# Preparing the second expert's weights one step a round beside the last chunk's lists, in an attention and mixture-of-experts kernel on one core

## The chip, the cores and the metric
The kernel runs on one core of one Trainium2 chip. The metric is the device time of one execution in microseconds (us), and lower is better. Before the change the median of three runs is 946.49 us (944.94 to 946.53).

## What is computed
The reference is linear attention without a softmax, a normalisation, and a mixture of eight experts of which every row uses two:

```python
kv  = einsum('bhsd,bhse->bhde', k, v)            # 8 batches, 8 heads, 576 rows, 64 wide
out = einsum('bhsd,bhde->bhse', q, kv)
out = out / sqrt(mean(out*out, -1) + 1e-6) * g_norm
x   = out as rows of 512, 4608 of them
noisy = x @ w_gate + log1p(exp(x @ w_noise)) * noise        # 8 logits a row
top2, top2_w = the two largest, softmax over these two
for e in range(8):                                          # w1[e] 512x1024, w2[e] 1024x512
    y[rows of e] += top2_w * (relu(x[rows of e] @ w1[e]) @ w2[e])
```

## The kernel before the change
**Two phases in one instruction stream.** The program is written out in full and every engine runs its instructions strictly in the order in which the Python code issues them (`tc.manual_schedule()`); engines meet at semaphores. In the first phase the attention goes tile by tile (36 tiles of 128 rows); the rows `x` are written to memory (`xs`) and the gate logits are worked out on the way. In the second phase the experts run as *units*: expert 0 has units 0 to 3 of two tiles (256 rows) and a tail, unit 4; every later expert has two units of four tiles (512 rows) and a tail. A unit is a gather of its rows by an indirect DMA from GpSimd (`gather`, L346), transposes into `xT` (`xpose`, L363; for units 0 to 4 by TensorE at L377, evicted by ScalarE at L380 and by VectorE at L381), a first layer (`l1`, L413; matmuls L426, evictions into `hT` by ScalarE L431 and VectorE L432) and a second layer (`l2`, L462; matmuls L470, eviction with the gate by ScalarE L501). Numbers are split into two fp16 halves, so each product takes three matmuls and each eviction writes a high half (ScalarE) and a low half (VectorE).

**Lists.** Which rows belong to an expert is found for chunks of 10, 18, 28 and 36 tiles. For a chunk, `gating` (L132) works out the top two on VectorE, ScalarE and GpSimd and counts rows with matmuls L176 and L178; `onehots` (L290) makes comparison matrices on VectorE (L296, L299, L302); `place` (L306) multiplies them on TensorE (L310); `finish` (L317) turns the result into indices. The units of expert 0 start before all chunks are there: units 0 to 2 (`EARLY` = 3) need only the first three chunks. `locate(1)` (L772) does the same for expert 1's list.

**Weights.** An expert's two weight matrices are loaded (`load_w1` L203, `load_w2` L208), and `weights` (L214) is a generator that prepares them step by step: four absolute-maximum reductions on VectorE (L221, one a step), then a diagonal `dg` (L228), a small fp32 matmul on TensorE that spreads it over the lanes (L232, which waits for `dg`), five short VectorE operations that make the scales (L234 to L241), and for each of four pieces a high half on ScalarE (L246, `w1h`) and a low half on VectorE (L250 and L252, `w1l`). All of this is done for w1 and then for w2. When w1 is split, the load of the next expert's w1 is issued into the same buffer.

**What sets the order around the change.** After the attention loop three things are stepped in rounds, `while side` (L800): `pump` advances the last chunk's lists, `fill_early` advances the early units (here the second layer of unit 1 and the first and second layer of unit 2), and `fill` (L790) advances the first generator of the deque `bg`. `bg` holds `locate(1)` and behind it `prepare(1)` (L763), which runs `weights(1)`. `locate(1)` yields without doing anything once three of its four parts are made, until the last chunk's lists are done, so that `prepare(1)` is not reached in these rounds. Behind the rounds come `finish` for expert 0's remaining tiles, the gathers of units 3 and 4 and their transposes, and then the units one by one.

```python
    bg.append(locate(1))
    bg.append(prepare(1))
    while side:
        pump()
        fill_early()
        fill()
    finish(0, M0, slice(2 * EARLY, CAP))
    gather(EARLY)
```

Of the kernel before, what the change touches and what calls it, by code (L numbers as in the profile page):

```python
# [51 lines left out]
def attention_moe(ctx: ExitStack, tc: tile.TileContext, kvm, kvr, qt, gn, wgn, noise, w1, w2, out):  # L52
# [155 lines left out]
    def load_w2(e):  # L208
        r = RW[e, 1] = late.get("raw", raw).tile([P, 4, 1024], F32, name="rw")
        v = w2[e].rearrange("(c f p) d -> c p f d", f=2, p=P)  # L210
        for c in range(4):
            SP.dma_start(r[:, c].rearrange("p (f d) -> p f d", f=2), v[c])
# [100 lines left out]
    def scale_gates(e, c):  # L313
        if "c" in WT.get(e, ()):
            V.tensor_scalar(LG[e][:, c], LG[e][:, c], WT[e]["c"], None, op0=OP.mult)

    def finish(e, M, c):  # L317
        m = lists.tile([P, 5, CAP], F32, name="m")
        V.tensor_copy(m, M.rearrange("p (v t) -> p v t", v=5))
        a = lists.tile([P, 2, CAP], F32, name="la")  # L320
        V.scalar_tensor_tensor(a[:, 0], m[:, 1], float(P), m[:, 0], op0=OP.mult, op1=OP.add)
        V.tensor_scalar(a[:, 1], m[:, 1], 0.0, lane, op0=OP.is_equal, op1=OP.mult)
        V.tensor_tensor(LI[e][:, c], a[:, 0, c], a[:, 1, c], OP.add)
        V.scalar_tensor_tensor(a[:, 0], m[:, 1], 0.0, sl[:, 1], op0=OP.is_gt, op1=OP.mult)  # L324
        V.tensor_tensor(a[:, 0], a[:, 0], sl[:, 0], OP.add)
        V.tensor_tensor(LS[e][:, c], LI[e][:, c], a[:, 0, c], OP.add)
        V.tensor_tensor(m[:, 2], m[:, 2], m[:, 3], OP.add)
        V.tensor_tensor(LG[e][:, c], m[:, 2, c], m[:, 4, c], OP.add)
        scale_gates(e, c)
# [16 lines left out]
    def gather(u):  # L346
        e, tiles, tail = units[u]
        for t in tiles:
            x = moe_a.tile([P, DM], F32, name="xg", bufs=GB)
            lim = {k // 2 - 1: m for m, k in MARKS.items()}.get(u, NT)  # L350
            src = xs[0:(1 + lim) * P, :]
            G.indirect_dma_start(out=x, out_offset=None, in_=src,  # L352
                                 in_offset=bass.IndirectOffsetOnAxis(ap=LI[e][:, t:t + 1], axis=0))
            XG[u, t] = x
# [179 lines left out]
    with tc.tile_pool(name="p1", bufs=2) as p1, tc.tile_pool(name="ps1", bufs=1, space=PSUM) as ps1:  # L534
# [138 lines left out]
        def pump():  # L673
            for it in list(side):
                it[0] -= 1
                while it[0] <= 0:
                    k = next(it[1], None)
                    if k is None:
                        side.remove(it)
                        break  # L680
                    it[0] = k

        def fill_early():
            while early:
                try:
                    next(early[0])
                    if held[0]:
                        scatter()
                    return
                except StopIteration:  # L690
                    early.popleft()
# [66 lines left out]
    bg = deque()  # L758
# [4 lines left out]
    def prepare(e):  # L763
        yield from weights(e, wts_b if e % 2 else wts_a)
        if e in ready:
            scale_gates(e, slice(0, CAP))
        loaded.add(e)
        if e + 1 < E:
            yield AFT
            load_w2(e + 1)  # L770

    def locate(e):  # L772
        M = psl.tile([P, 5 * CAP], F32, name="M")
        last = None
        for q in range(5):
            while q == 3 and side:
                yield 1
            oh = (yield from onehots(e, 9 * q, 9 * q + 9)) if q < 4 else None
            if q:
                place(M, last, q == 1, q == 4)  # L780
            last = oh
            yield PZ
        finish(e, M, slice(0, CAP))
        ready.add(e)
# [5 lines left out]
    def fill():  # L790
        hold[0] -= 1
        if bg and hold[0] <= 0:
            try:
                hold[0] = next(bg[0]) or 1
            except StopIteration:
                bg.popleft()

    bg.append(locate(1))
    bg.append(prepare(1))
    while side:  # L800
        pump()
        fill_early()
        fill()
    finish(0, M0, slice(2 * EARLY, CAP))
    gather(EARLY)
    held[0] = 1
# [148 lines left out]
```

## Time and profile before
| | |
|---|---|
| median of 3 runs | 946.49 us (944.94 to 946.53) |
| profiled execution: its own time | 947.06 us |
| profiled execution: span of the core | 945.3 us |
| TensorE (PE) matmuls busy | 902.0 us, 95% of the span |
| VectorE (DVE), ScalarE (ACT), GpSimd (POOL) busy | 450.0, 318.5, 365.3 us |
| chain that ended last, by engine | PE 23% (its longest engine) |

The profiled execution took 947.06 us, of which the span of 945.3 us is what its trace covers; all times in the trace count from the span's start. A share of busy time is an average over the whole run: the stretch that matters here lies between 160 and 240 us, from the end of the attention to the first unit of expert 1. A view called a timeline gives, for each row: start, duration, engine, line, operation, what it writes and reads, and in brackets how long the engine stood idle before it and what ended that.

### The profile page before, as it was taken

Reading aid. Unit: us, or ns where it says so; the run is one execution under the profiler, and the core shown is the slowest. Engines: PE = TensorE matmul, PEld = TensorE weight load, DVE = VectorE, ACT = ScalarE, POOL = GpSimd, SP = SyncE. Lnnn points to the kernel's source line nnn. Section 1 sums busy time; section 2 is a strip of 40 time slices with the busy share of each in tenths; the row PEclk is TensorE's granted clock in tenths of the full one; section 3 lists DMA queues with packets and bytes.
Section 4 is the critical chain, followed back from the end, with each engine's and each line's share of the span. In section 5 each row is a group of like instructions: output and inputs, shape, how many; then the busy total and the mean of one; then the engine's idle time right before and its main releaser. Section 6 shows DMA issues by size and latency. Waiting matters only on the chain. (4 is left out here: it accounts for less than half of the span.)

```text
span 945.3 us, 15846 instructions
## 1 busy us (share of the span) xinstructions
PE 902.0 (95%) x6436; PEld 510.0 (54%) x6436; DVE 450.0 (48%) x945; ACT 318.5 (34%) x511; POOL 365.3 (39%) x404
## 2 busy tenths in 40 slices
PE   9987989899999999999999999999999999999995
PEld 8876857665445544464445444644444445544453
DVE  1479858666644552634354445356364554321010
ACT  1654653225323332424133332332243323332111
POOL 0336435175235243335234433424333454243122
PEclk9986999999999999999999999999999999999998
DMA  8899895276836663387247744945358655353224
GB/s 330 334 406 373 318 390 206 96 135 171 188 72 101 158 187 68 67 169 197 41 95 117 216 79 100 180 116 109 74 146 145 152 112 62 52 113 58 34 39 57
DMA packets 123530, 143.28 MB, mean 152 GB/s; under 512 B 79632, under 2 KB 79760, under 8 KB 123408
## 3 DMA queue, kind: packets, MB, share of 16 engines
q1 hardware_dynamic: 100592, 90.11, 33.0%
q0 software_dynamic: 17920, 41.95, 23.2%
q10 hardware_dynamic: 4896, 9.44, 2.6%
q8 instruction: 94, 1.54, 0.7%
q14 instruction: 28, 0.23, 0.1%
HBM read 83.02 MB, written 40.11 MB: 130 GB/s over the span
## 5 line engine op out<-in xcount | busy, mean ns | idle before, releaser
L426 PE MATMUL pp<-xT,w1h 128*128 128x512 f16 (+5 forms) x1600 | 362.2, 323 | 6.6 <-DVE xT L381 2.2
L470 PE MATMUL pp<-w2h,hT 128*128 128x512 f16 (+1 forms) x1216 | 365.0, 376 | 1.7 <-ACT hT L431 1.7
L470 PEld LDWEIGHTS <-hT 128*128 128x128 f16 x1824 | 177.6, 98 | 205.7 <-issue 2.2
L432 DVE SCALAR_TENSOR_TENSOR hT<-pp,hT 128x512 f16<-128x512 f32 x160 | 107.8, 687 | 336.8 <-ACT hT L431 329.3
L404 POOL DMA_INDIRECT out_rows<-y,row x78 | 127.3, 1632 | 358.2 <-ACT y L501 350.2
L426 PE MATMUL pp<-xT,w1l 128*128 128x512 f16 (+5 forms) x800 | 253.3, 323 | 0.0
L470 PE MATMUL pp<-w2l,hT 128*128 128x512 f16 (+1 forms) x608 | 228.7, 376 | 0.0
L426 PEld LDWEIGHTS <-w1h 128*128 128x128 f16 x1600 | 148.7, 98 | 109.4 <-issue 5.4
L431 ACT ACTIVATE hT<-pp 128x512 f16<-128x512 f32 x160 | 92.4, 596 | 256.2 <-PE pp L426 246.6
L501 ACT ACTIVATE y<-pp,gate 128x512 f32<-128x512 f32 x77 | 52.1, 686 | 247.2 <-PE pp L470 189.9
L352 POOL DMA_INDIRECT xg<-xs,idx x80 | 83.0, 1038 | 80.8 <-DVE la L324 42.5
L426 PEld LDWEIGHTS <-w1l 128*128 128x128 f16 x800 | 78.5, 98 | 57.0 <-issue 2.4
L360 POOL TENSOR_TENSOR xh<-xg,xh 128x512 f16<-128x512 f32 x70 | 86.4, 1411 | 36.8 <-ACT xh L359 26.6
L221 DVE TENSOR_REDUCE mx<-rw 128x1 f32<-128x1024 f32 x64 | 74.7, 1209 | 2.1 <-DMA rw<-w 2.1
L594 PE MATMUL big<-kvw,qt 64*128 64x80 f32 (+1 forms) x640 | 46.0, 287 | 4.8 <-ACT kvw L584 4.8
L296 DVE TENSOR_TENSOR oa<-jb,lnb 128x1152 bf16<-128x1152 bf16 (+2 forms) x32 | 47.4, 1482 | 4.0 <-PE M L310 4.0
L594 PEld LDWEIGHTS big<-kvw,qt 64*128 64x128 f32 (+1 forms) x640 | 39.4, 190 | 11.0 <-ACT kvw L584 5.6
L359 ACT ACTIVATE xh<-xg 128x512 f16<-128x512 f32 x70 | 40.5, 623 | 12.7 <-DMA xg<-xs,idx 11.6
L403 POOL MEMSET tick<- 1x1 f32 x80 | 40.9, 512 | 0.0
L629 POOL TENSOR_TENSOR x<-o,ss 128x512 f32<-128x512 f32 x36 | 40.0, 1132 | 0.0
L611 DVE TENSOR_REDUCE ss<-sq 128x16 f32<-128x1024 f32 x18 | 21.9, 1217 | 36.9 <-ACT sq L609 36.9
L250 DVE SCALAR_TENSOR_TENSOR w1l<-rw,sc,w1h 128x1024 f16<-128x1024 f32 x24 | 29.8, 1279 | 19.8 <-ACT w1h L246 19.8
(139 smaller groups left out, 556.1 us busy)
## 6 DMA issues: line engine op xcount, KB each, us to landing
rw<-w SPq DMA_DIRECT2D x64, 512.0 KB
kvc<-kvm SPq DMA_DIRECT2D x32, 512.0 KB
xs<-x ACTq DMA_DIRECT2D x18, 512.0 KB
out_rows<-zrow SPq DMA_DIRECT2D x18, 512.0 KB
qt<-qt SPq DMA_DIRECT2D x8, 640.0 KB
qt<-qt SPq DMA_DIRECT2D x8, 512.0 KB
kvr<-kvr SPq DMA_DIRECT2D x4, 512.0 KB
xg<-xs,idx POOLq DMA_INDIRECT x80
```

The costliest lines, as they stand in the source:

```text
L221: V.tensor_reduce(mx[:, c:c + 1], src[:, c], axis=AX.X, op=OP.max, apply_absolute_value=True)
L296: V.tensor_tensor(oa, jb[:, None, :].to_broadcast([P, n, P]), lnb[:, s, e:e + 1].to_broadcast([P, n, P]), OP.is_equal)
L352: G.indirect_dma_start(out=x, out_offset=None, in_=src, in_offset=bass.IndirectOffsetOnAxis(ap=LI[e][:, t:t + 1], axis=0))
L360: G.tensor_tensor(x[:, 1], XG[u, t], x[:, 0], OP.subtract)
L403: G.memset(tick, 0.0)
L404: d = G.indirect_dma_start(out=out, out_offset=bass.IndirectOffsetOnAxis(ap=LS[e][:, t:t + 1], axis=0), in_=y, in_offset=None, compute_op= ...
L426: T.matmul(ps[:, f % ps.shape[1], 0:n], w[wn][:, c, f * P:(f + 1) * P], x[:, xo + c, 0:n], start=(c == 0 and k == 0), stop=(c == HP - 1 an ...
L431: A.activation(h[:, 0, f:f + nf, 0:n], ps, AF.Relu)
L432: V.scalar_tensor_tensor(h[:, 1, f:f + nf, 0:n], ps, 0.0, h[:, 0, f:f + nf, 0:n], op0=OP.max, op1=OP.subtract)
L470: T.matmul(ps, h[:, hk, f, i * P:(i + 1) * P], w[wn][:, f, d:d + n], start=(f == 0 and k == 0), stop=(f == 7 and k == 2))
L501: A.activation(y, pss[i][0] if tail else ps, AF.Copy, scale=LG[e][:, t:t + 1])
L594: T.matmul(TL[t][r0:r0 + n, h, hp * 80:(hp + 1) * 80], q[r, hp, s0 - o:s0 - o + n], KVW[b][r, hp], start=True, stop=True, skip_group_check ...
```

## The change
The generator of expert 1's weights gets a name, stays in the deque, and is stepped once in every round of `while side` (a step that asks for a pause of n rounds is followed after n rounds):

```diff
     bg.append(locate(1))
-    bg.append(prepare(1))
+    second_weights = prepare(1)
+    bg.append(second_weights)
+    wait = 0
     while side:
         pump()
         fill_early()
         fill()
+        wait -= 1
+        if wait <= 0:
+            wait = next(second_weights) or 1
     finish(0, M0, slice(2 * EARLY, CAP))
     gather(EARLY)
```

No instruction is added or dropped; instructions change places. Three places matter.

TensorE, in the second layer of unit 1, where the counting matmuls (L176) of the last chunk stand between two groups of L470:

```order
 L470 LDWEIGHTS hT
 L470 MATMUL pp<-w2h,hT 128x512
+L232 MATMUL pp<-dg,onef 128x128 [waits DVE_49]
 L176 LDWEIGHTS ones
-L176 MATMUL RM<-gt_sel,ones 128x64 [waits DVE_49]
+L176 MATMUL RM<-gt_sel,ones 128x64
 L176 LDWEIGHTS ones
 L176 MATMUL RM<-gt_sel,ones 128x56
```

The small matmul of w1's scale now stands ahead of the counting matmuls; it stood in the first layer of unit 3 before.

VectorE, at the same time: the last chunk's top two (L163 to L167, and ahead of these rows L146 to L158) and then its lists. `rw` is the loaded weight matrix, `mx`, `sc`, `dg` and `al` belong to its scale:

```order
 L167 RECIPROCAL gt_d<-gt_d 128x8 [waits DVE_49]
+L221 TENSOR_REDUCE mx<-rw 128x1 [waits DMAHW5_49]
+L223 TENSOR_REDUCE sc<-mx 128x1 [waits DVE_49]
+L225 TENSOR_SCALAR sc<-sc,gabs 128x1 [waits DVE_49]
+L228 TENSOR_SCALAR dg<-ident,sc 128x128 [waits DVE_49]
 L296 TENSOR_TENSOR oa<-jb,lnb 128x1152
 L179 CAST vals<-ge 128x64 [waits Pool_49]
 L299 TENSOR_TENSOR ot<-tb_101,t_115 128x90
```

The reduction shown is the fourth; the first stands ahead of L146, the second behind L299, the third behind L302, all of them ahead of L167. The six scale operations L234 to L241 follow behind the last row shown, ahead of the first L381 of unit 2's `xT`, and a first L250 stands ahead of the second L381. On ScalarE two L246 stand between the two L380 of unit 2.

VectorE, at the end of the rounds, between the last `hT` of unit 2's first layer and `finish`, before the change:

```order
L302 TENSOR_TENSOR ob<-ot,vals 128x450 [waits DVE_49]
L432 SCALAR_TENSOR_TENSOR hT<-pp,hT 128x512 [waits Activation_49] x3
L296 TENSOR_TENSOR oa<-jb,lnb 128x1152
L319 COPY m<-RM 128x50
L321 SCALAR_TENSOR_TENSOR la<-m 128x10 [waits DVE_49]
```

and after it:

```order
L302 TENSOR_TENSOR ob<-ot,vals 128x450 [waits DVE_49]
L432 SCALAR_TENSOR_TENSOR hT<-pp,hT 128x512 [waits Activation_49] x2
L221 TENSOR_REDUCE mx<-rw 128x1 [waits DMAHW1_49]
L432 SCALAR_TENSOR_TENSOR hT<-pp,hT 128x512 [waits Activation_49]
L221 TENSOR_REDUCE mx<-rw 128x1 [waits DMAHW2_49]
L296 TENSOR_TENSOR oa<-jb,lnb 128x1152
L221 TENSOR_REDUCE mx<-rw 128x1 [waits DMAHW3_49]
L319 COPY m<-RM 128x50
```

Two reductions of w2 are new between the last L432 and L319, the copy with which `finish` begins; a third stands ahead of that L432.

The small matmul of w2's scale moves from behind the second layer of unit 3 into the first layer of unit 3, and the rest of w2's preparation moves ahead of unit 5 with it. The load of expert 2's w1, behind the transposes of unit 5 on the sync queue before, now stands ahead of them, and follows the last L252 of expert 1's w1.

## Rows read from the trace of the kernel before
**Rows 1.** The page, first part: busy time of each engine, its share of the span, instructions.
```profile
PE 902.0 (95%) x6436; PEld 510.0 (54%) x6436; DVE 450.0 (48%) x945; ACT 318.5 (34%) x511; POOL 365.3 (39%) x404
```
**Rows 2.** The waits of TensorE over the whole run: waiting engine, tile and line, releaser, us in total, times, longest.
```profile
PE pp L232 <- DVE dg L228: 6.1, 7, 2.3
```
**Rows 3.** Timeline of TensorE, 187 to 240 us: the two scale matmuls of expert 1.
```profile
211.77 0.46 PE L232 MATMUL pp<-dg,onef 128*128 128x128 f32 x2 [0.23 <-DVE dg L228]
212.07 0.38 PE L426 MATMUL pp<-xT,w1h 128*128 128x256 f16 x2
...
232.19 0.46 PE L232 MATMUL pp<-dg,onef 128*128 128x128 f32 x2 [2.26 <-DVE dg L228]
```
**Rows 4.** Timeline of TensorE, 169 to 175 us: the end of unit 1's second layer and the start of unit 2's first.
```profile
169.08 0.35 PE L176 MATMUL RM<-gt_sel,ones 128*128 128x64 bf16 x8
...
170.40 0.38 PE L470 MATMUL pp<-w2h,hT 128*128 128x512 f16 x1
...
171.05 0.39 PE L310 MATMUL M<-ob,oa 128*128 128x50 bf16 x9
172.53 0.27 PE L426 MATMUL pp<-xT,w1h 128*128 128x256 f16 x1 [1.09 <-ACT xT L380]
174.99 0.27 PE L426 MATMUL pp<-xT,w1h 128*128 128x256 f16 x1 [2.20 <-DVE xT L381]
```
**Rows 5.** Timeline of VectorE, 165 to 181 us.
```profile
165.05 0.23 DVE L146 SCALAR_TENSOR_TENSOR gt_nl<-zl,gt_w 128x64 f32<-128x64 f32 x1 [0.61 <-POOL gt_w L144]
...
168.81 0.21 DVE L167 RECIPROCAL gt_d<-gt_d 128x8 f32<-128x8 f32 x1
168.93 1.31 DVE L296 TENSOR_TENSOR oa<-jb,lnb 128x1152 bf16<-128x1152 bf16 x1
171.26 0.20 DVE L179 CAST vals<-ge 128x64 bf16<-128x64 f32 x1 [1.01 <-POOL ge L172]
171.37 0.25 DVE L299 TENSOR_TENSOR ot<-tb,t 128x90 bf16<-128x90 bf16 x1
172.02 0.69 DVE L381 TENSOR_TENSOR xT<-pp,xT 128x512 f16<-128x512 f32 x1 [0.41 <-ACT xT L380]
...
174.26 0.68 DVE L381 TENSOR_TENSOR xT<-pp,xT 128x512 f16<-128x512 f32 x1
...
180.91 1.36 DVE L296 TENSOR_TENSOR oa<-jb,lnb 128x1152 bf16<-128x1152 bf16 x1 [4.00 <-PE M L310]
```
**Rows 6.** Timeline of VectorE, 209 to 232 us: the preparation of expert 1's weights where it stands before the change.
```profile
209.55 1.21 DVE L221 TENSOR_REDUCE mx<-rw 128x1 f32<-128x1024 f32 x1
...
211.23 0.40 DVE L228 TENSOR_SCALAR dg<-ident,sc 128x128 f32<-128x128 f32 x1
...
214.99 0.28 DVE L234 TENSOR_REDUCE al<-pp 128x1 f32<-128x128 f32 x1
...
215.87 0.16 DVE L241 SCALAR_TENSOR_TENSOR sc<-sc,g 128x1 f32<-128x1 f32 x1
...
223.24 2.47 DVE L250 SCALAR_TENSOR_TENSOR w1l<-rw,sc,w1h 128x1024 f16<-128x1024 f32 x2
225.63 1.27 DVE L252 SCALAR_TENSOR_TENSOR w1l<-rw,sc,w1h 128x1024 f16<-128x1024 f32 x1
226.83 4.59 DVE L221 TENSOR_REDUCE mx<-rw 128x1 f32<-128x1024 f32 x4
```
**Rows 7.** Timeline of ScalarE: unit 1's last eviction and unit 2's `xT` at 171 us, and four pieces of a weight matrix's high half.
```profile
170.81 0.69 ACT L501 ACTIVATE y<-pp,gate 128x512 f32<-128x512 f32 x1 [3.83 <-PE pp L470]
171.40 1.08 ACT L380 ACTIVATE xT<-pp 128x512 f16<-128x512 f32 x2
...
233.58 4.26 ACT L246 ACTIVATE w2h<-rw,sc 128x1024 f16<-128x1024 f32 x4 [2.93 <-DVE sc L238]
```
**Rows 8.** Busy time in stretches: bounds and length in us, then for each engine busy time and instructions, then the granted TensorE clock (1.00 is 2.4 GHz, 0.50 is 1.2 GHz), the DMA share and GB/s; and from the timeline of TensorE the wait inside the first of them.
```profile
136.00:140.00 4.00, 3.35 (x28) 2.16 (x29) 1.85 (x14) 1.36 (x4) 0.00 (x0) 1.00 1.05 404
176.00:178.00 2.00, 2.00 (x13) 1.49 (x11) 0.80 (x3) 0.00 (x0) 0.00 (x0) 0.57 0.00 0
178.00:180.00 2.00, 2.00 (x13) 1.48 (x11) 0.00 (x0) 0.60 (x1) 0.00 (x0) 0.58 0.00 0
...
136.65 0.66 PE L377 MATMUL pp<-ident,xg 128*128 128x128 f32 x4 [2.34 <-DVE xT L381]
```
**Rows 9.** From the list of the last `hT` of unit 2 to the first transpose of unit 3: timelines of VectorE, GpSimd and TensorE, and two stretches of 1 us.
```profile
188.29 0.69 DVE L432 SCALAR_TENSOR_TENSOR hT<-pp,hT 128x512 f16<-128x512 f32 x1 [2.13 <-ACT hT L431]
...
190.16 0.20 DVE L319 COPY m<-RM 128x50 f32<-128x50 f32 x1
...
191.68 0.99 POOL L352 DMA_INDIRECT xg<-xs,idx  x1 [16.95 <-DVE m L327]
...
195.46 0.60 PE L377 MATMUL pp<-ident,xg 128*128 128x128 f32 x4
...
193.00:194.00 1.00, 1.00 (x7) 0.44 (x5) 0.84 (x7) 0.69 (x1) 0.93 (x1) 1.00 0.66 94
194.00:195.00 1.00, 1.00 (x6) 0.45 (x5) 0.91 (x3) 0.00 (x0) 0.77 (x1) 1.00 0.67 213
```
**Rows 10.** Timelines of GpSimd and TensorE at 121 and 129 us: a gather while the DMA engines are loaded, and the transpose that waits for it.
```profile
121.22 0.99 POOL L352 DMA_INDIRECT xg<-xs,idx  x1 [4.17 <-DVE la L324]
...
129.47 0.63 PE L377 MATMUL pp<-ident,xg 128*128 128x128 f32 x4 [0.98 <-DMA xg<-xs,idx]
```

## The prediction
> **What bounds the kernel now.** I read the page first: TensorE is busy for 902.0 us, 95% of the span [rows 1]. So a microsecond is won only where TensorE waits, and any new wait of TensorE is lost in full unless it takes the place of another. The waits of TensorE come next: seven waits of the scale matmul L232 for `dg` take 6.1 us in all [rows 2]. Its timeline shows the two of them that belong to expert 1, 0.23 us and 2.26 us [rows 3]. These 2.49 us are all that the change can aim at, since they are the price of expert 1's weights being prepared late. Then I read the place to which the work goes, on TensorE [rows 4], VectorE [rows 5] and ScalarE [rows 7]. There TensorE runs from the counting matmuls at 169.08 without a gap to 171.05 and then waits twice, 1.09 and 2.20 us, for unit 2's `xT`; VectorE, which writes half of `xT`, has gaps of only 0.61, 1.01 and 0.41 us up to the second L381 and one of 4.00 us behind it. The reader is to see that the vector engine, not TensorE, is the scarce one in these 10 us, and that the free time lies behind the place where it is wanted.
>
> **Term 1: the wait at the moved L232.** TensorE takes its matmuls in the order of the program, so the matmul that waits for `dg` holds the counting matmuls and the rest of unit 1 behind it. When is `dg` there? One reduction costs (4.59 - 1.21) / 3 = 1.13 us from start to start [rows 6]. Three stand ahead of L167, so L167 comes 3.39 us later, less the 0.61 us that VectorE waits for GpSimd at L146 anyway [rows 5]: 2.78 us. The fourth starts where L296 started, 168.93 + 2.78 = 171.71. From the start of such a reduction to the end of `dg` it took 211.23 + 0.40 - 209.55 = 2.08 us [rows 6], so `dg` ends at 173.79, and the matmul follows 0.14 us later (211.63 to 211.77 [rows 3, 6]), at 173.93. TensorE is there at 169.08 [rows 4]: a wait of **4.85 us**. L232 itself holds it 0.30 us (211.77 to 212.07 [rows 3]). The stream stands 5.15 us later.
>
> **Term 2: unit 2's `xT`.** Unit 1's last eviction on ScalarE, at 170.81 right behind the last L470 [rows 4, 7], goes to 175.96, the first L380 to 176.55, and the first L381 from 172.02 to 177.17. VectorE is free by then: behind `dg` it has L296 (some 1.3 us), two short operations and the six scale operations, 1.04 us (214.99 to 216.03 [rows 6]), which ends at about 176.3. Between the two L381 lay 2.24 us of work [rows 5]; a first L250 joins it, 1.20 us ((225.63 - 223.24) / 2 [rows 6]). The second L381 starts at 177.17 + 2.24 + 1.20 = 180.61. ScalarE's two L246 ahead of the second L380 cost 2 x 1.07 us [rows 7] and let it end at about 179.8, which is not later. TensorE followed the second L381's start after 0.73 us (174.26 to 174.99 [rows 4, 5]): 181.34 in place of 174.99. Terms 1 and 2 together: **+6.35 us**. The old `xT` wait of 3.29 us is inside this figure; it becomes about 4.8 us.
>
> **Term 3: the clock.** After the waits of [rows 4] the granted clock was 0.57 and 0.58 from 176 to 180 us, that is 1.2 GHz most of the time, while TensorE was busy throughout [rows 8]; this costs about 4 x 0.42 = 1.7 us now. After a wait of 2.34 us at 136.65 it stayed at 1.00 [rows 8]. Now there are two waits of nearly 5 us. Between them lie about 2.35 us of work (169.08 to the end of L310, 171.44 [rows 4]), and what of it runs at half speed delays the `xT` chain by as much; the low stretch after the second wait I keep as it was. Bounds: 0, and 2.35 for the work between plus 1.7 for a low stretch of twice the length. I take **+1.4 us**, a good half of the work between, because in the row the clock fell only 1 to 2 us after TensorE had resumed.
>
> The Trainium skill (TensorE: Matmul & The Clock Gate, section What's actually happening) has the engine at half rate after an idle stretch until it has been busy for a while. By that rule all work between the two waits would be at half speed, and this sum would come out about 1 us higher; the row of a clock that fell after the work had resumed speaks for less.
>
> **Term 4: unit 3's gather.** `finish` for expert 0's last tiles started 1.87 us after the last `hT` of unit 2 [rows 9], which follows TensorE. Two reductions between add 2.26 us; the gather, 1.52 us after L319 now, comes as much later against TensorE. Does TensorE notice? A tile is 128 x 512 x 4 bytes, 0.262 MB; 0.094 and 0.213 MB had come by 194 and 195 us, so the first tile was there at about 194.8, and TensorE took it at 195.46 without a wait: 0.66 us to spare [rows 9]. Left: **+1.6 us** (bounds 0 and 2.26).
>
> **Term 5: what is won.** The 0.23 and the 2.26 us go. The L232 of w2 moves into unit 3's first layer, behind two of its four blocks. Its `dg` then hangs on the last reduction, which stands right behind the evictions of unit 4, so I expect the old 0.2 us there again. Net **-2.3 us** (bounds -2.49 and -1.5). What stands late next is unit 5's `xT`, from the gather, the halves and the transposes behind it; these shift with TensorE and their weights' pieces on ScalarE now come earlier, so I charge nothing. The other three pieces of `w1l` (3.6 us) lie in VectorE's 4.00 us gap [rows 5] and are charged nothing; without that gap they would add to term 4. Expert 2's w1 load goes out some 8 us ahead of unit 3's gather and is through by then; if not, it is the third rival.
>
> **Sum.** 6.35 + 1.4 + 1.6 - 2.3 = **+7.05 us**. The profiled execution took 947.06 us, so 954.1; the median of the runs lies 0.57 us lower, so the forecast is 953.5 us. The bounds of the terms give 6.35 - 2.49 = +3.9 (950.4) and 6.35 + 4.05 + 2.26 - 1.5 = +11.2 (957.7).
>
> **Rivals.**
> *Cover, faster.* The added vector work might fit into VectorE's gaps, so that `dg` is there when TensorE comes and only the 2.49 us go: 944.0 us. For it: from 165 to 181 us VectorE stands idle for 6.0 us in four gaps [rows 5], as long as four reductions and a `w1l` piece. Against it: only 0.61 us of it lies ahead of L167. It decides from the point where `dg` ends before 169.08; by my working it is 4.7 us late. 4%.
> *Exchange, the same time.* The wait at L232 could simply take the place of the old wait for `xT`, since unit 2's first transpose is already done by then: 5.15 - 3.29 = +1.9, less 2.3, gives 946.1 us. It needs both L381 to run ahead of the scale operations and the first L250, and in the order of VectorE they stand behind them. 6%.
> *Collision, slower still.* Expert 2's w1 load, 2 MB, now follows the last L252 of w1. If that comes late, the load meets the gather of unit 3. A gather under load took from 121.22 to 129.4, 8.2 us, in place of the 3.1 us from 191.68 to 194.8 [rows 9, 10]: up to 5 us more on TensorE, about 958.6 us. 8%.
> *Mild.* Terms 1, 2 and 5 hold, but the clock and the gather cost nothing: 950.5 us. 17%, inside the range.
>
> **How the numbers follow.** The forecast with its terms 3 and 4 has 65%, the mild case 17%, collision 8%, exchange 6%, cover 4%. The range, 949.5 to 958.0, takes in the forecast and the mild case with the bounds of their terms and a little on either side; the rest is left out. Within 0.2% (1.9 us), which is about what a measurement of this kernel can tell from no change, lie exchange and little else: 6%. Faster by more: 4%. Slower by more: 90%.
>
> **What would show it.** In the changed profile TensorE should wait 4 to 6 us at L232 near 169 us with VectorE's `dg` as the releaser, then 4 to 5 us more for unit 2's `xT`; the granted clock should be low in parts of 173 to 187 us; a wait of 1 to 2 us for the gather should stand at unit 3's first transpose; and the 2.26 us ahead of unit 5 should be gone. The prediction is wrong if TensorE waits less than 2 us at the moved L232, or if the waits are there and the stretch up to unit 5 is still no longer than before.

## The result and the profile after

The changed kernel takes 955.01 us in the median of five runs (954.09 to 957.26), against 946.49 us for the kernel before; the ratio is 1.0089, interval [1.0066, 1.0112]. The forecast was 953.5 us in a range of 949.5 to 958.0. The profiled execution took 954.27 us (span 952.5 us), 7.2 us more than the profiled execution before; the forecast sum was 7.05.

First the page, which shows why shares alone do not help here: TensorE's share of busy time is what it was in [rows 1].

```profile
PE 903.2 (95%) x6436; PEld 509.1 (53%) x6436; DVE 456.3 (48%) x945; ACT 319.0 (33%) x511; POOL 366.4 (38%) x404
```

The waits of TensorE over the run (in us in total, times, longest) show the new ones. The first row answers to [rows 2].

```profile
PE pp L232 <- DVE dg L228: 8.4, 6, 4.4
...
PE pp L426 <- ACT xT L380: 3.2, 1, 3.2
```

The timeline of TensorE gives their places. The first row is a transpose ahead of all moved work, the second the moved L232, the third a transpose between the two pauses, the next two are unit 2's `xT` (they answer to [rows 4]), the sixth is unit 3's gather (before: the row at 195.46 in [rows 9], without a wait), the last is unit 3's first layer, which waited 1.91 us before too. What releases that last wait is not shown: L327, which the bracket names, stands behind the same matmul in the trace of before (203.49 against 202.15). The bracketed wait of 2.26 us of [rows 3] has no counterpart: from 212 to 319 us TensorE waits for nothing.

```profile
166.89 0.60 PE L377 MATMUL pp<-ident,xg 128*128 128x128 f32 x4
...
173.15 0.80 PE L232 MATMUL pp<-dg,onef 128*128 128x128 f32 x2 [4.36 <-DVE dg L228]
...
176.44 0.60 PE L377 MATMUL pp<-ident,xg 128*128 128x128 f32 x4
...
180.43 0.37 PE L426 MATMUL pp<-xT,w1h 128*128 128x256 f16 x1 [3.16 <-ACT xT L380]
182.02 0.37 PE L426 MATMUL pp<-xT,w1h 128*128 128x256 f16 x1 [1.22 <-DVE xT L381]
...
204.87 0.63 PE L377 MATMUL pp<-ident,xg 128*128 128x128 f32 x4 [1.72 <-DMA xg<-xs,idx]
...
211.89 0.38 PE L426 MATMUL pp<-xT,w1h 128*128 128x256 f16 x2 [2.12 <-DVE m L327]
```

The timeline of VectorE shows who makes TensorE wait. In [rows 5] L167 stood at 168.81 and L296 followed it at once. Now three reductions stand ahead of L167 and a fourth behind it, and `dg` ends at 173.10. The second L381 starts at 181.28, where it started at 174.26. (This trace runs 0.46 us ahead of the one of before when the change sets in, which the table below takes out.)

```profile
163.90 1.22 DVE L221 TENSOR_REDUCE mx<-rw 128x1 f32<-128x1024 f32 x1
...
166.22 1.21 DVE L221 TENSOR_REDUCE mx<-rw 128x1 f32<-128x1024 f32 x1
...
169.18 1.21 DVE L221 TENSOR_REDUCE mx<-rw 128x1 f32<-128x1024 f32 x1
...
171.04 0.21 DVE L167 RECIPROCAL gt_d<-gt_d 128x8 f32<-128x8 f32 x1
171.16 1.17 DVE L221 TENSOR_REDUCE mx<-rw 128x1 f32<-128x1024 f32 x1
...
172.81 0.29 DVE L228 TENSOR_SCALAR dg<-ident,sc 128x128 f32<-128x128 f32 x1
...
181.28 0.68 DVE L381 TENSOR_TENSOR xT<-pp,xT 128x512 f16<-128x512 f32 x1
```

The view by stretches (bounds and length, busy time and instructions of PE, PEld, DVE, ACT, POOL, then the granted TensorE clock, DMA share and GB/s) answers to [rows 8]. The clock is low in most of the work between the two pauses (L232 and 174 to 176) and again behind the second; behind the pause of 2.12 us at 211.89 it stays at 1.00.

```profile
172.00:174.00 2.00, 0.85 (x8) 0.79 (x9) 1.90 (x5) 0.00 (x0) 0.43 (x2) 0.71 0.10 38
174.00:176.00 2.00, 2.00 (x13) 0.82 (x11) 1.48 (x9) 0.00 (x0) 0.30 (x1) 0.50 0.00 0
...
182.00:184.00 2.00, 1.98 (x10) 1.39 (x10) 2.00 (x2) 0.45 (x1) 0.00 (x0) 0.50 0.00 0
184.00:186.00 2.00, 2.00 (x11) 1.36 (x10) 2.00 (x4) 0.00 (x0) 0.00 (x0) 0.50 0.00 0
186.00:188.00 2.00, 2.00 (x19) 1.68 (x17) 0.12 (x1) 0.60 (x1) 0.00 (x0) 0.88 0.00 0
...
212.00:214.00 2.00, 2.00 (x20) 1.79 (x19) 2.00 (x4) 0.00 (x0) 1.60 (x2) 1.00 0.99 135
```

To see where the time goes, the same instruction is looked up in both traces. The attention takes a little longer or shorter from one profile to the next; so the common start is the first transpose L377 of unit 2, ahead of all moved work: 167.35 us before, 166.89 after, that is 0.46 us earlier. The last column is the difference with this 0.46 us added.

| place | before | after | later by |
|---|---|---|---|
| TensorE, the counting matmuls L176 | 169.08 | 173.73 | 5.11 |
| TensorE, unit 2's first layer running (second L426 row) | 174.99 | 182.02 | 7.49 |
| ScalarE, unit 2's first L501 | 193.07 | 200.59 | 7.98 |
| TensorE, unit 3's first layer | 202.15 | 211.89 | 10.20 |
| ScalarE, L501 behind the second layer of unit 3 | 229.97 | 238.95 | 9.44 |
| ScalarE, L501 after the old 2.26 us wait | 258.82 | 265.31 | 6.95 |
| ScalarE, L501 in expert 1 | 292.22 | 297.67 | 5.91 |
| ScalarE, last L501 | 933.47 | 940.71 | 7.70 |

The lateness grows to 10.20 us within 39 us of the moved L232 (173.15 to 211.89). By 300 us 4.3 us of it are given back, and the later experts add 1.8 us again.

### The profile page after: what moved, and what is told of

It reads as the page before. It is cut to its first block, busy times and chain, and to the rows that moved or that the text cites. A ratio compares the mean times of both kernels' runs of the same rounds, so it can differ in the third digit from the quotient of the medians.

```text
span 952.5 us, 15850 instructions
## 1 busy us (share of the span) xinstructions
PE 903.2 (95%) x6436; PEld 509.1 (53%) x6436; DVE 456.3 (48%) x945; ACT 319.0 (33%) x511; POOL 366.4 (38%) x404
## 3 DMA queue, kind: packets, MB, share of 16 engines
q10 hardware_dynamic: 4896, 9.44, 2.6%
## 5 line engine op out<-in xcount | busy, mean ns | idle before, releaser
L426 PE MATMUL pp<-xT,w1h 128*128 128x512 f16 (+5 forms) x1600 | 362.8, 323 | 7.7 <-ACT xT L380 3.2
L470 PE MATMUL pp<-w2h,hT 128*128 128x512 f16 (+1 forms) x1216 | 365.8, 377 | 1.8 <-ACT hT L431 1.4
L470 PEld LDWEIGHTS <-hT 128*128 128x128 f16 x1824 | 177.9, 98 | 206.5 <-issue 3.6
L432 DVE SCALAR_TENSOR_TENSOR hT<-pp,hT 128x512 f16<-128x512 f32 x160 | 108.1, 688 | 346.0 <-ACT hT L431 346.0
L426 PE MATMUL pp<-xT,w1l 128*128 128x512 f16 (+5 forms) x800 | 253.6, 323 | 0.0
L470 PE MATMUL pp<-w2l,hT 128*128 128x512 f16 (+1 forms) x608 | 229.3, 377 | 0.0
L426 PEld LDWEIGHTS <-w1h 128*128 128x128 f16 x1600 | 148.6, 98 | 112.2 <-issue 9.2
L501 ACT ACTIVATE y<-pp,gate 128x512 f32<-128x512 f32 x77 | 52.1, 686 | 264.6 <-PE pp L470 211.1
L426 PEld LDWEIGHTS <-w1l 128*128 128x128 f16 x800 | 78.5, 98 | 56.2 <-issue 1.5
L352 POOL DMA_INDIRECT xg<-xs,idx x80 | 80.5, 1006 | 68.4 <-DVE la L324 27.1
L360 POOL TENSOR_TENSOR xh<-xg,xh 128x512 f16<-128x512 f32 x70 | 90.3, 1469 | 31.3 <-ACT xh L359 31.3
L296 DVE TENSOR_TENSOR oa<-jb,lnb 128x1152 bf16<-128x1152 bf16 (+2 forms) x32 | 49.7, 1554 | 2.3 <-PE M L310 2.3
L250 DVE SCALAR_TENSOR_TENSOR w1l<-rw,sc,w1h 128x1024 f16<-128x1024 f32 x24 | 30.1, 1298 | 19.8 <-ACT w1h L246 19.8
```

Source lines behind the costliest of these rows:

```text
L296: V.tensor_tensor(oa, jb[:, None, :].to_broadcast([P, n, P]), lnb[:, s, e:e + 1].to_broadcast([P, n, P]), OP.is_equal)
L352: G.indirect_dma_start(out=x, out_offset=None, in_=src, in_offset=bass.IndirectOffsetOnAxis(ap=LI[e][:, t:t + 1], axis=0))
L360: G.tensor_tensor(x[:, 1], XG[u, t], x[:, 0], OP.subtract)
L426: T.matmul(ps[:, f % ps.shape[1], 0:n], w[wn][:, c, f * P:(f + 1) * P], x[:, xo + c, 0:n], start=(c == 0 and k == 0), stop=(c == HP - 1 an ...
L432: V.scalar_tensor_tensor(h[:, 1, f:f + nf, 0:n], ps, 0.0, h[:, 0, f:f + nf, 0:n], op0=OP.max, op1=OP.subtract)
L470: T.matmul(ps, h[:, hk, f, i * P:(i + 1) * P], w[wn][:, f, d:d + n], start=(f == 0 and k == 0), stop=(f == 7 and k == 2))
```

## The experiments

Each ratio is to the kernel before, run on the same chip. A shift is the lateness against the trace of before, from the common start of the table above, which lies between 166.46 and 169.24 us in these traces. Shifts come from one profiled execution each, ratios from several executions, so the two need not agree to a microsecond or two.

**1. w1 alone beside the lists.** Does the loss come from w1's part?

```diff
-        if wait <= 0:
+        if wait <= 0 and "half" not in WT.get(1, ()):
             wait = next(second_weights) or 1
```

> The change, but the generator is stepped in the rounds only until w1 is split; w2's reductions no longer stand ahead of the list of unit 3. Theory (each wait of TensorE has its own cause, and the 1.72 us for unit 3's gather come from the reductions of w2 ahead of the list): that wait goes, everything else stays, about 953.3 us, 6.8 us above the kernel before. Rival (the gather is late only because the whole stretch is, or its wait hides a later one): 955 us as the change.

Measured: 955.38 us, ratio 1.0068 [1.0044, 1.0091]. The timeline of TensorE has the first wait unchanged and no wait for the gather, as expected of w2's reductions; the view by stretches shows what took its place.

```profile
173.40 0.80 PE L232 MATMUL pp<-dg,onef 128*128 128x128 f32 x2 [4.36 <-DVE dg L228]
...
209.87 0.48 PE L426 MATMUL pp<-xT,w1h 128*128 128x256 f16 x2 [1.92 <-POOL tick L403]
```
```profile
210.00:212.00 2.00, 2.00 (x11) 1.41 (x10) 1.79 (x11) 0.82 (x2) 1.60 (x2) 0.57 1.01 125
212.00:214.00 2.00, 2.00 (x13) 1.48 (x11) 1.93 (x3) 0.00 (x0) 1.72 (x3) 0.58 1.01 132
```

Unit 3 starts 7.9 us late instead of 10.2, so the gather's wait does come from w2's reductions. But the clock then falls to 0.57 behind unit 3's pause of 1.92 us, where it stays at 1.00 in the change (pause of 2.12 us), and at the next L501 (224.79 us before) both traces are 9.4 us late. The wait was real; whether taking it away shortens the run is open: the interval holds the theory's 6.8 us (1.0072) and the change's 1.0089 alike, and the trace ends 8.2 us late, where the change ends 7.7 us late.

**2. L232 later, behind four more steps.** This keeps the vector work in front and takes the matmul out of TensorE's way.

```diff
-            for _ in range(2 + slack):
+            for _ in range(2 + slack + gap):
                 yield
...
-    second_weights = prepare(1)
+    second_weights = prepare(1, 4)
```

> The change, with four more pauses between dg and the scale matmul L232, for both matrices: L232 then stands behind unit 1's second layer, and the scale operations and all low halves stand behind both xT evictions. The reductions stay ahead of the last chunk's top two. Theory (vector work in front of what TensorE needs is the cause, and the place of L232 is only a part): no wait at L232, but 2.2 us at the counting matmuls L176 for the top two and about 3.9 us for xT, the stretch up to unit 2 some 3.0 us later than before in place of 7.5; with the gather no longer late, 948.6 us. Rival (the place of the matmul is all of it): TensorE waits no more than before, 945.8 us or less.

Measured: 950.15 us, ratio 1.0015 [0.9993, 1.0036], within what the theory asked for (1.0022). The rival's 945.8 us would be 0.9993, the very edge of the interval; TensorE's new waits of 2.19 and 3.04 us speak against it. Of the theory's places the first is met (2.19 us at the counting matmuls), `xT` takes 2.59 us in place of 3.9, and unit 2 starts 2.98 us late as expected. The gather, which was to be in time, is not. Timelines of TensorE, of VectorE (the last `hT` of unit 2), of the sync queue and of GpSimd, and two stretches:

```profile
170.54 0.35 PE L176 MATMUL RM<-gt_sel,ones 128*128 128x64 bf16 x8 [2.19 <-DVE gt_sel L165]
...
177.08 0.37 PE L426 MATMUL pp<-xT,w1h 128*128 128x256 f16 x1 [2.59 <-DVE xT L381]
...
201.57 0.63 PE L377 MATMUL pp<-ident,xg 128*128 128x128 f32 x4 [3.04 <-DMA xg<-xs,idx]
...
191.76 1.28 DVE L432 SCALAR_TENSOR_TENSOR hT<-pp,hT 128x512 f16<-128x512 f32 x2
...
191.88 1.76 SPq L206 DMA_DIRECT2D rw<-w  x4
...
195.75 0.99 POOL L352 DMA_INDIRECT xg<-xs,idx  x1 [18.93 <-DVE m L327]
...
172.00:174.00 2.00, 2.00 (x17) 1.70 (x15) 1.93 (x6) 1.59 (x3) 0.09 (x1) 0.50 0.00 0
...
196.00:198.00 2.00, 2.00 (x11) 0.94 (x10) 1.74 (x11) 0.67 (x1) 1.69 (x2) 1.00 1.00 401
```

Without L232 in the way TensorE still waits 2.19 us, now for the counting operand itself: the reductions hold up the list on VectorE. So the wait of 4.36 us splits into 2.2 us for the reductions ahead of L167 and 2.2 us for the reduction and the scale behind it, for which only L232 waits. I had not foreseen the 3.04 us. The low pieces of w1 stand ahead of the last two `hT`, so that the gather goes out 4.96 us late (195.75) where unit 2's first L501 is 3.79 us late. And it goes out into expert 2's w1 load, which was issued from 191.88 on (401 GB/s from 196 to 198 us): from its issue to the transpose it takes 5.82 us (195.75 to 201.57), against 3.42 us in the change (201.45 to 204.87). This is the prediction's rival of a collision, in a version in which the gather follows the load sooner.

**3. Filler ahead of two pauses.** Sixty matmuls of zeros ahead of the moved L232 and as many ahead of unit 2's first layer keep TensorE busy.

```diff
+            if e == 1 and o == 0:
+                keep_warm(60)
             ps = ps_tile([P, P])
...
+        if u == EARLY - 1:
+            keep_warm(60)
```

> The change, with 60 small matmuls on zeros, whose result nothing reads, on TensorE ahead of the moved L232 and 60 more ahead of unit 2's first layer, so that both waits are filled with work and the clock can stay up. Theory (the clock adds 2 to 3 us of its own: 1.3 us in the work between the two waits, which delays xT, and 0.8 to 1.6 us behind the second): granted clock 1.00 from 170 to 190 us, 952.5 us. Rival (the low clock falls on time that TensorE waits anyway, only the part behind the second wait counts): 954.2 us.

Measured: 957.04 us, ratio 1.0078 [1.0054, 1.0101]: not below the change, so the expectation failed for the whole. For its place it did not. The timeline of VectorE (its lines stand two further down than in the change):

```profile
174.50 0.29 DVE L228 TENSOR_SCALAR dg<-ident,sc 128x128 f32<-128x128 f32 x1
...
181.54 0.68 DVE L383 TENSOR_TENSOR xT<-pp,xT 128x512 f16<-128x512 f32 x1
```

From the start of `dg` to the start of the second `xT` it takes 7.04 us; in the change it took 8.47 (172.81 to 181.28). At the full clock the work between the pauses is 1.43 us shorter, and unit 2's first L501 comes 3.45 us earlier than in the change (shift 4.53 against 7.98). The clock then fell behind unit 3's pause (0.50 in the stretch below), as in experiment 1, and from 287 us on nothing of the gain is left (shift 6.41 against 6.14). The trace ends 9.88 us late, where the change ends 7.70 us late; what costs the later part is not shown.

```profile
212.00:214.00 2.00, 2.00 (x11) 1.44 (x10) 1.06 (x1) 0.00 (x0) 1.66 (x4) 0.50 0.95 143
```

**4. Late start.** The generator starts 15 rounds later, with the four steps of experiment 2.

```diff
-    wait = 0
+    wait = 15
```

> The change, but the generator is first stepped in the 15th round, behind unit 2's xT, and has four more pauses between dg and L232: w1's reductions fall into the vector engine's gaps beside unit 2's first layer, nothing of the weights stands between the last hT and the list of unit 3, and w2 keeps its place behind w1. Theory (only the place of the vector work was wrong; the aim, 2.49 us at the two scale matmuls, can be had): no new wait, the two old ones gone, 944.0 us. Rival (the vector engine has no free time there either, so that hT or the list comes late): 946.5 us or more.

Measured: 946.02 us, ratio **0.9965 [0.9948, 0.9983]**: this version beats both kernels. The theory's 944.0 us, a ratio of 0.9974, lies in the interval; the rival's 946.5 us or more (1.0000) does not. Timelines of TensorE and of VectorE (the last `hT` of unit 2), and a stretch:

```profile
174.41 0.27 PE L426 MATMUL pp<-xT,w1h 128*128 128x256 f16 x1 [1.08 <-ACT xT L380]
176.88 0.27 PE L426 MATMUL pp<-xT,w1h 128*128 128x256 f16 x1 [2.20 <-DVE xT L381]
197.09 0.63 PE L377 MATMUL pp<-ident,xg 128*128 128x128 f32 x4 [1.25 <-DMA xg<-xs,idx]
...
204.16 0.38 PE L426 MATMUL pp<-xT,w1h 128*128 128x256 f16 x2 [2.28 <-POOL tick L403]
...
190.29 0.68 DVE L432 SCALAR_TENSOR_TENSOR hT<-pp,hT 128x512 f16<-128x512 f32 x1
...
176.00:178.00 2.00, 1.12 (x11) 1.01 (x11) 2.00 (x5) 0.00 (x0) 0.30 (x1) 1.00 0.00 0
```

The two waits for `xT` are those of [rows 4] to a hundredth, no L232 of expert 1 waits, and the shift is -2.5 us from 286 us to the end. The prediction's bound for what could be won was 2.49 us, but this agreement has some luck in it. From unit 3's first layer (shift 0.13) to 258.82 us (-3.04), where the two L232 of expert 1 stood with their waits, the trace does win 3.2 us. Ahead of that two things cancel. The clock stays at 1.00 behind the two pauses, where it fell in [rows 8], which puts unit 2's first L501 1.67 us early. And "no new wait" failed: the reductions and `dg` hold up the last `hT` (the rival's mechanism; with the common start it is 0.1 us later than before, although TensorE is 1.67 us ahead), so that TensorE waits 1.25 us for the gather and then 2.28 us in place of 1.91. Behind 258.82 us 0.57 us are lost again by 287 us. That the kept clock belongs to this version, and not to the one execution that was profiled, is not shown.

**5. The later experts' order restored.** Four steps of rest ahead of expert 2's list put every instruction from there on in the order of the kernel before.

```diff
+        if e == 2:
+            yield 4
```

> The change, with four steps of rest ahead of expert 2's list, so that from expert 2 on VectorE and TensorE take their instructions in the order of the kernel before again. Theory: in the change the shift against before is +5.45 us (+5.9 with the start of the profile set even) behind expert 1 and +7.2 (+7.7) at the end; the 1.8 us between come from the background work of the later experts, which stands four steps earlier against the tiles, so that the scale matmul L232 and its evictions are met at worse places. With the order restored this growth goes: 1.3 to 1.8 us less than the change, about 953.4 us or a ratio of 1.0057 to before (948 to 949 on this chip), and the shift stays within 0.3 us from 300 us to the end. Rival: the growth comes from the units' later start against the transfers, and not from the order: then the ratio stays at the change's 1.009 and the shift grows again by 1.3 us or more.

Measured: 954.99 us, ratio 1.0080 [1.0051, 1.0108]. The time cannot tell it from the change. In the trace the shift is 5.81 us at 292 us (places in the time of before) and 5.83 at 434 us, where the change has grown from 5.91 to 7.64; at 636 us it is 6.41 against 7.99, at the end 6.63 against 7.70. So 1.1 to 1.8 us of the lateness in the later experts come with the order. The growth of 0.8 us that is left, where at most 0.3 was expected, stays open. A gain of 1.1 us at the end is too small to be told from none by these ratios, which differ by 0.0009.

**6 and 7. Two reductions fewer, one more.** A dose on the first term.

```diff
-                V.tensor_reduce(mx[:, c:c + 1], src[:, c], axis=AX.X, op=OP.max, apply_absolute_value=True)
+                n = 64 if e == 1 and o == 0 and c in (1, 2) else 1024
+                V.tensor_reduce(mx[:, c:c + 1], src[:, c, 0:n], axis=AX.X, op=OP.max, apply_absolute_value=True)
```

> The change with two of the four moved reductions of expert 1's w1 (the second and third quarter) cut to 64 columns of 1024; it leaves out most of those quarters from the scale's maximum. Theory: the wait at the moved L232 is the sum of the reductions ahead of dg, so it falls by two times 1.13 less two short operations of about 0.15 us, 1.96 us, from 4.36 to about 2.4 us. If a wait of that length still brings the half clock for the work behind it, the whole is 2.0 us shorter than the change; if the clock stays at 1.00 there, 3.3 us shorter. Ratio to before 1.0055 to 1.0070. Rival: the wait hangs on GpSimd's L146 or on the load of the weights: then it stays above 4 us and the time stays at the change's 1.008 to 1.009.

```diff
-                V.tensor_reduce(mx[:, c:c + 1], src[:, c], axis=AX.X, op=OP.max, apply_absolute_value=True)
+                for _ in range(2 if e == 1 and o == 0 and c == 0 else 1):
+                    V.tensor_reduce(mx[:, c:c + 1], src[:, c], axis=AX.X, op=OP.max, apply_absolute_value=True)
```

> The change with the first moved reduction of expert 1's w1 made twice into the same column. Theory: the wait at L232 grows by one reduction, 1.13 us, from 4.36 to 5.5 us, xT of unit 2 and everything behind it comes 1.1 us later, and the whole is 1.1 us longer than the change: ratio to before 1.0095 to 1.0105. Rival: VectorE has slack ahead of L167, or the later wait for xT takes the added time up: the wait at L232 grows by less than 0.6 us or the waits for xT shrink by as much, and the time stays at 1.008 to 1.009.

Measured: 952.98 us, ratio 1.0061 [1.0039, 1.0082], for two fewer; 957.20 us, ratio 1.0117 [1.0094, 1.0139], for one more. The six executions with two fewer lie between 951.28 and 954.38 us, the six with one more between 956.03 and 960.07 us on the same chip, with the change's 1.0089 between the two ratios. So the time follows the dose from end to end; each single step is about as large as its interval, and the upper one is larger than expected (1.0095 to 1.0105). Both rivals (L146 or the load; slack on VectorE) fall by the waits at L232. With two fewer, TensorE's timeline and two stretches read:

```profile
172.41 0.49 PE L233 MATMUL pp<-dg,onef 128*128 128x128 f32 x2 [2.35 <-DVE dg L229]
...
178.25 0.37 PE L427 MATMUL pp<-xT,w1h 128*128 128x256 f16 x1 [3.16 <-ACT xT L381]
```
```profile
172.00:174.00 2.00, 1.59 (x16) 1.04 (x17) 1.97 (x6) 0.00 (x0) 0.19 (x1) 1.00 0.34 131
174.00:176.00 2.00, 1.10 (x15) 0.87 (x14) 1.07 (x7) 1.53 (x3) 0.12 (x1) 1.00 0.02 6
```

With one more:

```profile
174.52 0.79 PE L233 MATMUL pp<-dg,onef 128*128 128x128 f32 x2 [5.33 <-DVE dg L229]
...
182.03 0.37 PE L427 MATMUL pp<-xT,w1h 128*128 128x256 f16 x1 [2.59 <-ACT xT L381]
```
```profile
174.00:176.00 2.00, 1.48 (x13) 1.14 (x14) 1.97 (x6) 0.00 (x0) 0.08 (x1) 0.50 0.00 0
```

The wait at L232 goes 2.35, 4.36, 5.33 us: 2.01 us for two reductions and 0.97 for one, close to the sum of durations. With one more, the first wait for `xT` gives 0.57 us back, and the shift at unit 2's first L501 is 8.80 us against 7.98. Behind 2.35 us the clock stays at 1.00 in the work that follows, behind the longer two it is 0.50. That is why unit 2's first L501 comes 3.4 us earlier with two fewer (shift 4.62), and not 2.0.

**8. Filler ahead of three pauses, order restored.** Experiments 3 and 5 together, with 30 more matmuls ahead of unit 3's first layer (the edit is shown against experiment 3).

```diff
-        if u == EARLY - 1:
-            keep_warm(60)
+        if u in (EARLY - 1, EARLY):
+            keep_warm(60 if u < EARLY else 30)
```

> The change with matmuls of zeros in three of TensorE's new or old pauses: 60 ahead of the moved L232, 60 ahead of unit 2's first layer, 30 ahead of unit 3's, and the four steps of rest ahead of expert 2's list. Each filler is shorter than its pause, so no wait becomes longer. Theory: the half clock behind the two new pauses costs 3.4 us in the change (in the kernel with the first two fillers alone unit 2 ended 3.45 us earlier than in the change, and lost it again at a half clock behind unit 3's pause); with the third filler it is kept. Profile: granted clock 1.00 from 160 to 230 us. Time 3 to 4 us below the change, ratio to before 1.0045 to 1.006. Rival: what a high clock wins is given back at waits for VectorE and the transfers: ratio 1.0075 or more.

Measured: 955.92 us, ratio 1.0097 [1.0075, 1.0119]: the rival's figure, but not by its mechanism. In its place the theory held: the granted clock is 1.00 from 170 to 218 us (stretch below), unit 2's first L501 is 4.5 us late (experiment 5: 8.1), and the shift is a constant 3.5 us from 286 us to 508 us of before (experiment 5: 5.8, then 6.2). Then TensorE loses 4.1 us in two pauses that the kernel before does not have, and for neither does the trace show a wait for VectorE or a transfer; a stretch and the timeline:

```profile
170.00:218.00 48.00, 41.90 (x435) 32.96 (x433) 36.24 (x92) 12.82 (x19) 18.63 (x25) 1.00 0.50 115
...
521.21 1.01 PE L474 MATMUL pp<-w2h,hT 128*128 128x512 f16 x2 [2.42 <-issue]
...
665.56 0.38 PE L474 MATMUL pp<-w2h,hT 128*128 128x512 f16 x1 [1.69 <-issue]
```

"Issue" means that nothing in the profile is waited for. What holds TensorE there is not shown; 150 matmuls had been added to its stream ahead of these places, and the change without them has a pause of 0.39 us at the first of the two. An experiment that adds instructions is thus no clean subtraction over the whole run, and I read this one only up to there.

## Why the prediction was right, point by point

**Term 1, the wait at L232: right.** Forecast 4.85 us, measured 4.36, with `dg` as the releaser. (The forecast counts from the start of the matmul that stood there, the bracket from the end of the one before it; counted as the forecast counts, from 169.08 to 173.61 with the common start, it is 4.53.) From the common start L167 came 2.69 us later (forecast 2.78), `dg` ended at 173.56 (173.79), and the counting matmuls, which stand behind L232, started 5.11 us later (5.15). L232 held TensorE 0.58 us (to 173.73) and not the 0.30 us of the full clock, which made up for the shorter wait. The dose of experiments 6 and 7 confirms the price of a reduction, and experiment 2 which part of it only L232 waits for.

**Term 2, unit 2's `xT`: right.** Terms 1 and 2 were to give 6.35 us. Measured are 7.49, which contain 1.43 us of clock by experiment 3, so 6.06 us.

**Term 3, the clock: its first part right by luck, its second left out.** I took +1.4 us, bounds 0 and 4.05. The work between the pauses cost 1.43 us more. But I had counted on a clock that falls 1 to 2 us after TensorE has resumed, so that the work would begin fast. It was the other way round: L232, the first matmul behind the pause, already took 0.80 us (0.46 in [rows 3]), and L377 at 176.44 took 0.60 again, as ahead of the pause. So the work began slow and ended fast, and the share came out the same. The low stretch behind the second pause, which I kept as it was, costs more too: by unit 2's first L501 the shift has grown from 7.49 to 7.98. Together 1.9 us. The rule of the Trainium skill (TensorE: Matmul & The Clock Gate, section What's actually happening) that the engine runs at half rate after an idle stretch until it has been busy for a while agrees with the 0.50 behind the 4.36 us. The extra 1 us that the prediction derived from it did not come, since the clock was back before the work between the pauses ended.

**Term 4, unit 3's gather: the wait right, its neighbourhood left out.** Forecast +1.6 us, measured a wait of 1.72 us. The shift grows by 2.22 us up to unit 3's first layer, since the wait there is 0.21 us longer than before and 0.29 us more are spread between. The timeline of the sync queue puts the load of expert 2's w1 at 191.01; the stretch from 200 to 202 us moves 2 GB/s, and the gather goes out at 201.45. So the load was over, and the rival of a collision (8%) did not come in the change. It was near: in experiment 2, where the gather goes out 3.9 us behind the load's first issue and not 10.4, it came.

```profile
191.01 2.70 SPq L206 DMA_DIRECT2D rw<-w  x4
...
201.45 0.99 POOL L352 DMA_INDIRECT xg<-xs,idx  x1 [19.92 <-DVE m L327]
...
200.00:202.00 2.00, 2.00 (x11) 0.94 (x10) 1.74 (x12) 0.69 (x1) 0.55 (x1) 1.00 0.01 2
```

**Term 5, what is won: the sum right, its parts wrong.** I had -2.3 us. Between unit 3 and 259 us the shift falls by 3.25 us: the 0.23 and 2.26 us, the 0.30 us of L232 itself that leaves unit 3 (which I had forgotten to take back), and 0.46 us that no bracket accounts for (some 0.3 us of it may lie in how the two brackets count: from the end of a matmul that lasts 0.38 us, where the next usually starts after 0.22). A further 1.04 us go with a pause of L310 at 261.52 us in the trace of before (row below). What causes it is not shown: it is there in experiments 2 and 4 too, and not in 1 and 5 to 8. Against this stand 1.8 us in the later experts, at L232 waits such as the 0.84 us at 319.69 in the change. I had charged later experts nothing; experiment 5 shows that the changed order behind expert 1 is part of it. Net -2.5 us. The two omissions have opposite signs, and their cancelling was luck.

```profile
261.52 0.20 PE L310 MATMUL M<-ob,oa 128*128 128x50 bf16 x1 [1.02 <-issue]
```

**Sum.** 6.06 + 1.92 + 2.22 - 3.25 - 1.04 + 1.79 = 7.70 us from the common start, less the 0.46 us by which this profile was ahead there: 7.24, against +7.05. The terms of the clock, of the gather and of the later experts were too small by 0.5, 0.6 and 1.8 us; terms 1 and 2 were 0.3 us too large, and the omissions in term 5 gave 2.0 back. The last 0.46 us that bring the sum so close are chance: so far this execution was ahead before any moved work began. So the mechanism and its large terms were right, the agreement to 0.2 us was luck. The ratio of the medians says 8.4 us, with an interval of 6.2 to 10.6.

**The rivals.** *Cover* (VectorE's gaps take the work): ahead of L167 the gaps took in 0.7 us of 3.4. It was wrong for this place; for a later start no wait at L232 of expert 1 is left (experiment 4). *Exchange*: the old wait for `xT` of 3.29 us did not go, it became 4.38. *Mild*: excluded by the clock and the gather's wait.

## What to carry to other kernels

An engine with 48% load over the run can still be the scarce one in the 10 us to which work is moved: add up its gaps ahead of the instruction that the bounding engine waits for, not over the stretch. A matmul that waits for a vector chain holds everything behind it on TensorE, so place it by when its operand is ready; the same steps, started 15 rounds later and with four more between `dg` and L232, turned +0.9% into -0.35%. And when a new wait appears, look at the clock behind it and at the pauses after it before counting what its removal would give.

## What had not been expected of the hardware

The length of a pause alone did not decide whether the clock fell behind it. After pauses of 1.09 and 2.20 us ahead of unit 2's first layer it was 0.57 before the change [rows 4, 8], and after 1.08 and 2.20 us at the same instructions it stayed at 1.00 in experiment 4. After 1.92 us (experiment 1, at 209.87) it fell to 0.57, after 2.12 us at the same instruction in the change it stayed at 1.00; after 2.19 us (experiment 2, at 170.54) the stretch from 172 to 174 us had 0.50, after 2.35 us (experiment 6) it stayed at 1.00. In experiments 1 and 3, which took a pause away, the clock was low behind unit 3's pause, where it is 1.00 in the change, and that gave back what had been won up to there. Whether the one caused the other, and what besides the length of a pause makes the difference, was not isolated.
